# Turning z by VectorE blocks and strided reads in a two-layer FNet/GEGLU kernel

## The chip, the cores and the metric

The kernel runs on one core of a Trainium2 chip. The metric is the device time of one execution, in microseconds (us); the median of three runs is given, and the profile is one execution on its own. Below, TensorE (PE) multiplies matrices, VectorE (DVE) and ScalarE (ACT) work on elements, GpSimd (POOL) does small work and issues stores, and SyncE (SP) issues loads.

## The reference

The input x is 2048 rows (tokens) of 512 values, float32. Four residual sublayers follow each other: mix, GEGLU, mix, GEGLU, with the same matrices in both rounds.

```
def A(x):      # mix: real part of a two-dimensional DFT, as matrix products
    a = x @ dft_hid_re.T ;  b = x @ dft_hid_im.T
    return dft_seq_re @ a - dft_seq_im @ b
def B(x):      # GEGLU, 512 -> 1792 -> 512
    return (gelu(x @ w_gate) * (x @ w_up)) @ w_down
x = x + A(layernorm(x));  x = x + B(layernorm(x))      # twice
```

## The kernel before

**Products.** A float32 product is made of three fast ones: each operand is split into a high part (copied by ScalarE, line 110) and a rest (subtracted by VectorE, line 111), and `mm3` (lines 144 to 146) adds high x high, high x low and low x high in PSUM. The large products use one level of Strassen's scheme (in Winograd's form), so operands also come as sums and differences of quarters (S1 to S4, T1 to T4).

**Tiles.** All SBUF data lives in 102 slots of 128x512 float32 (`sb.get`, `sb.put`, first in, first out), and PSUM in 8 such slots (`ps8`). Activations lie in DRAM between layers as 16 tiles of 128 rows.

**Order.** A Tile scheduler places the instructions of each engine, starting from the order in which the program issues them; on the chip each engine then runs its list in order. Two lists in the program matter here:

- The *stream*: matrix tiles in the order of use. `take()` gives the next item, keeps items split 5 ahead (`AHEAD`) and loads issued 4 further ahead (`RAW`), all on SyncE's queue (line 210).
- The *queue*: small steps of side work. `step()` runs one after each stream item of a mix (six matmuls) or each down product of a GEGLU pass (twelve matmuls).

**Mix** (layers 0 and 2). Row blocks b of 512 rows pass through the stages A11, A12, S2, S3, A22 (`six`, six matmuls an item; S2 and S3 have 16 items each, the others 8), and the hidden DFT (`hid_groups`). In the last row block the order is S2, S3, A22 and then the hidden groups.

**GEGLU** (layers 1 and 3). Two passes w of 1024 rows each. A pass multiplies the transposed rows z^T (as blocks B11, B21, B22, T1 to T4, all split) by the gate and up weights in 14 steps, `up`. The down products of the pass's first 512 rows lag six steps behind; then come the last six of those and fourteen for its second 512 rows.

**Around the change.** `block_steps(layer, w)` makes the steps that prepare z^T for a pass: eight `norm(i)` steps (lines 368 to 384: statistics and scale on VectorE, a power on GpSimd, z on ScalarE), four `first(c)` and four `second(c)` steps that turn 128 columns of z each by TensorE (line 454: four 128x128 transposes into one PSUM slot, with an identity), copy and split the result and form differences, and ten steps that form T4 and split T1 to T4. For the first pass they enter the queue at S3 of the mix's last row block (line 606), for the second pass after the first half of the first pass's down products (line 876). A loop at the end of the pass (line 887) empties the queue, two steps per product where needed.

Of the kernel before, what the change touches and what calls it, by code (L numbers as in the profile page):

```python
# [38 lines left out]
def fnet_geglu(ctx: ExitStack, tc: tile.TileContext, x_in, ws, wh, wgu, wdn, out):  # L39
# [73 lines left out]
    def split_slot(src):  # L113
        hi, lo = sb.get(F32R), sb.get(F32R)
        split(src, hi, lo)
        return hi, lo
# [20 lines left out]
    def copied(src):  # L137
        v = sb.get()
        nc.scalar.activation(v, src, AF.Copy)  # L139
        return v  # L140
# [227 lines left out]
    def normed(layer, i):  # L368
        x = fresh.pop(i, None)
        if x is None:  # L370
            x = x_load(layer, i)
        st = spool.tile([P, 6], F32, name="st")
        nc.vector.bn_stats(st, x)  # L373
        mv = spool.tile([P, 2], F32, name="mv")
        nc.vector.bn_aggr(mv, st)
        rstd = spool.tile([P, 1], F32, name="rstd")
        nc.vector.tensor_scalar_add(rstd, mv[:, 1:2], EPS)  # L377
        nc.gpsimd.tensor_tensor(rstd, rstd, power, op=ALU.pow)  # L378
        shift = spool.tile([P, 1], F32, name="shift")
        nc.vector.scalar_tensor_tensor(shift, mv[:, 0:1], -1.0, rstd, op0=ALU.mult, op1=ALU.mult)  # L380
        z = sb.get()
        nc.scalar.activation(z, x, AF.Identity, bias=shift, scale=rstd)  # L382
        sb.put(x)
        return z
# [55 lines left out]

    def block_steps(layer, w):

        z, t = {}, {}

        def norm(i):
            def run():
                z[i] = normed(layer, w * 2 * NT + i)
            return run

        def turned(c, part):  # L450

            ps = ps8.get()
            for i in range(NT):
                nc.tensor.transpose(ps[:, i * P:(i + 1) * P], z[part * NT + i][:, c * P:(c + 1) * P], ident)  # L454
            if c == ND - 1:
                sb.put(*(z.pop(part * NT + i) for i in range(NT)))
            return ps

        def difference(a, b):
            v = sb.get()  # L460
            minus(v, a, b)
            return v

        def first(c):
            def run():
                ps = turned(c, 0)
                t[f"B{1 + c // 2}1", c % 2] = copied(ps)
                blocks[f"B{1 + c // 2}1", c % 2] = split_slot(ps)
                ps8.put(ps)
            return run  # L470

        def second(c):
            def run():
                ps = turned(c, 1)
                if c < 2:
                    t["B12", c] = copied(ps)
                    t["T1", c] = difference(ps, t["B11", c])
                    sb.put(t.pop(("B11", c)))
                else:
                    c0 = c - 2  # L480
                    t["T2", c0] = difference(ps, t["T1", c0])
                    t["T3", c0] = difference(ps, t["B12", c0])
                    sb.put(t.pop(("B12", c0)))
                    blocks["B22", c0] = split_slot(ps)
                ps8.put(ps)
            return run

        def fourth(c):
            def run():
                t["T4", c] = difference(t["B21", c], t["T2", c])  # L490
                sb.put(t.pop(("B21", c)))
            return run

        def divide(name, c):
            def run():
                blocks[name, c] = split_slot(t[name, c])
                sb.put(t.pop((name, c)))
            return run

        one = [norm(i) for i in range(NT)] + [first(c) for c in range(ND)]  # L500
        two = [norm(i) for i in range(NT, 2 * NT)] + [second(c) for c in range(ND)]
        two += [fourth(c) for c in range(2)]
        two += [divide(name, c) for name in ("T2", "T3", "T1", "T4") for c in range(2)]
        return one + two


    def mix(layer):
# [70 lines left out]
                    cs[0, c] = v  # L578
            ps8.put(*side)

        chains, sides, us, ws4 = {}, {}, {}, {}

        def s2(b):
            last, fore = b == NB - 1, b < FORE[layer]
            if fore:
                chains[b] = [ps8.get() for _ in range(2)]
                if b:
                    sums[b] = [fetched((layer, b, c)) for c in range(2)]
                    cs.update({(0, c): fetched((layer, b, c, "sum")) for c in range(2)})
            chain, side = chains[b], [ps8.get() for _ in range(2)]  # L590
            sides[b] = side
            if last and layer == 0:
                queue.extend(weight_steps(0))
            for second, k in skewed():
                if second:
                    six(side, "T1", k, k == 0, k == NK - 1, "T12" if last else None)
                else:
                    six(chain, "T2", k, fore and k == 0, k == NK - 1)
            us[b] = [based(b, c, p) for c, p in enumerate(chain)]
            ws4[b] = [based(b, c, p) for c, p in enumerate(side)]  # L600

        def s3(b):
            last = b == NB - 1
            chain, side, u, w4 = chains[b], sides.pop(b), us.pop(b), ws4.pop(b)
            if last:
                queue.extend(block_steps(layer + 1, 0))
                if layer == 0:
                    queue.extend(weight_steps(1))
            for second, k in skewed():
                if second:  # L610
                    six(side, "B22", k, False, k == NK - 1, "2" if last else None)
                else:
                    six(chain, "T3", k, False, k == NK - 1)
                if not second and k == NK - 1:
                    for c in range(2):
                        plus(w4[c], w4[c], chain[c])
                        cs[1, 2 + c] = w4[c]
            for c in range(2):
                plus(u[c], u[c], side[c])
                cs[0, 2 + c] = u[c]  # L620
            ps8.put(*side)
# [32 lines left out]
    def weight_steps(n):  # L654

        src, v = [], {}

        def load():
            src.extend(sb.get() for _ in range(4))
            for i, names in enumerate((*pieces[:3], ("S4", "A21"))):  # L660
                for name, h in zip(names, half):
                    v[name] = src[i][:, h]
            with tc.issue_after(stream["last"].ins):
                nc.sync.dma_start(src[0], wgu[n, :, :512])
                nc.sync.dma_start(v["A22"], wgu[n, :, 512:768])
                nc.sync.dma_start(v["A21"], wgu[n, :, 768:])

        def sums():
            plus(v["S1"], v["A21"], v["A22"])
            minus(v["S2"], v["S1"], v["A11"])  # L670
            minus(v["S3"], v["A11"], v["A21"])
            minus(v["S4"], v["A12"], v["S2"])

        def divide(i):
            def run():
                to = wblocks[n][:, i * 1024:min((i + 1) * 1024, 7 * 512)]
                p = wparts.setdefault(n, {"tiles": []})
                if i < 3:
                    t = split_slot(src[i])
                    kept(to, t)  # L680
                    for name, h in zip(pieces[i], half):
                        p[name] = (t[0][:, h], t[1][:, h])
                else:
                    t = (split_side(v["S4"]),)
                    nc.gpsimd.dma_start(to, f32(t[0]))
                    p["S4"] = (t[0][:, half[0]], t[0][:, half[1]])
                p["tiles"] += t
                sb.put(src[i])
            return run

        return [load, sums] + [divide(i) for i in range(len(pieces))]
# [36 lines left out]
    def geglu(w, layer):  # L728
# [46 lines left out]
        def first(n):  # L775
            if n < NF:
                chain[n] = ps8.get()
                product(n, chain[n], "A11", "B11", True, True)
                c11[n] = copied(chain[n])
# [85 lines left out]
        for bc in list(blocks):  # L865
            sb.put(*blocks.pop(bc))
        load_rows(0)
        if before_mix:
            queue.extend((lambda k=k: first_rows(layer + 1, k)) for k in range(NK))
        for f in range(NF - LAG, NF):  # L870
            down(f, 0)
# [1 line left out]
        if w == 0:  # L873
            weight_load(0)
            weight_load(1)
            queue.extend(block_steps(layer, 1))
        elif before_mix:
            for k in range(NT):
                queue.append(lambda k=k: second_rows(layer + 1, k))
                queue.append(lambda k=k: combine(k))  # L880
            queue.extend((lambda k=k: combine_late(k)) for k in range(NT))
# [102 lines left out]
```

## Time and profile before

| | |
|---|---|
| median of three runs | 1668.8 us (1666.82 to 1669.08) |
| the profiled execution | 1666.76 us |
| its span, first to last instruction | 1664.9 us |
| granted TensorE clock | 0.998 |
| DMA, mean | 233 GB/s |

The profile is of one execution. A row of the groups reads: line, engine, operation, output <- inputs, shape, count | busy us, mean ns of one | idle time of the engine before them and what ended it. In a timeline, the brackets give the idle time ahead of the instruction. In the table of stages, each engine's busy time is followed by its number of instructions; then come the granted clock, the mean busy share of the 16 DMA engines and GB/s. SPq is SyncE's queue of DMA issues.

### The profile page before, as it was taken

What the parts mean: (1) busy time and instruction counts of PE and PEld (TensorE: products, weight loads), DVE (VectorE), ACT (ScalarE), POOL (GpSimd) and SP (SyncE); (2) the same over time, 40 slices, a digit from 0 to 9 for tenths busy, and PEclk for the clock granted to TensorE, in tenths of its full rate; (3) what the DMA queues carried; (4) which work ended last, traced back from release to release, by engine and by line L of the source; (5) the groups of instructions that cost most, each with busy time, mean ns of one, the idle gap of its engine ahead of it and who ended that gap; (6) DMA issues with size and microseconds to landing.
All of it is one profiled execution on the core that took longest, in us unless ns stands there. A gap on an engine that the chain in (4) does not pass through costs nothing.

```text
span 1664.9 us, 22527 instructions
## 1 busy us (share of the span) xinstructions
PE 1650.4 (99%) x7296; PEld 1359.2 (82%) x7296; DVE 1190.7 (72%) x2132; ACT 776.2 (47%) x1352; POOL 169.3 (10%) x288
## 2 busy tenths in 40 slices
PE   9999999999999999999999999999999999999999
PEld 6877788888788888888888888888888888888887
DVE  8997978687887765655898785857946556656561
ACT  7744434255565543534663333444635443444440
POOL 3212100021422110000210000000100000100000
PEclk9999999999999999999999999999999999999999
DMA  9788886778766876555665766565695559755551
GB/s 361 247 279 329 306 317 227 253 252 291 273 229 215 292 269 233 172 189 198 216 227 182 240 228 228 168 227 188 225 386 184 171 177 321 259 178 175 186 183 51
DMA packets 200726, 388.46 MB, mean 233 GB/s; under 512 B 23840, under 2 KB 27424, under 8 KB 200608
## 3 DMA queue, kind: packets, MB, share of 16 engines
q1 hardware_dynamic: 183168, 329.86, 59.1%
q0 software_dynamic: 17440, 57.16, 9.1%
q8 instruction: 58, 0.95, 0.2%
q14 instruction: 60, 0.49, 0.1%
HBM read 328.73 MB, written 58.20 MB: 232 GB/s over the span
## 4 chain that ended last, share of the span: by engine, by line
PE 93%; DVE 3%; DMA 2%; issue 1%; ACT 1%; SPq 0%; DVEq 0%; ACTq 0%
PE p L144 31%; PE p L145 30%; PE p L146 30%; DMA s<-wgu 2%; DVE s L111 1%; PE p L551 1%; PE p L454 1%; DVE s L135 1%; DMA s<-ws 1%; DVE s L132 1%; DMA s<-x 0%; DVE s L725 0%; DVE s L739 0%; DVE s L723 0%; ACT s L110 0%
## 5 line engine op out<-in xcount | busy, mean ns | idle before, releaser
L145 PE MATMUL p<-s,s 128*128 128x512 f32 x2368 | 921.7, 390 | 1.9 <-DVE s L111 1.9
L146 PE MATMUL p<-s,s 128*128 128x512 f32 x2368 | 908.6, 390 | 0.0
L144 PE MATMUL p<-s,s 128*128 128x512 f32 x2368 | 901.2, 391 | 7.0 <-DVE s L135 3.9
L110 ACT ACTIVATE s<-s 128x512 fp32r<-128x512 f32 (+1 forms) x758 | 438.0, 617 | 467.6 <-DVE s L132 98.6
L111 DVE TENSOR_TENSOR s<-s,s 128x512 fp32r<-128x512 f32 (+1 forms) x758 | 490.2, 679 | 87.1 <-ACT s L110 64.3
L144 PEld LDWEIGHTS p<-s,s 128*128 128x128 f32 x2368 | 445.0, 188 | 102.9 <-DVE s L135 5.0
L145 PEld LDWEIGHTS p<-s,s 128*128 128x128 f32 x2368 | 445.4, 188 | 95.0 <-DVE s L111 3.1
L146 PEld LDWEIGHTS p<-s,s 128*128 128x128 f32 x2368 | 445.2, 188 | 93.7 <-DVE s L111 0.7
L135 DVE TENSOR_TENSOR s<-s,p 128x512 f32<-128x512 f32 x316 | 213.0, 685 | 188.9 <-PE p L146 140.6
L139 ACT ACTIVATE s<-p 128x512 f32<-128x512 f32 x248 | 145.2, 593 | 187.4 <-PE p L146 171.4
L132 DVE TENSOR_TENSOR s<-s,s 128x512 f32<-128x512 f32 (+1 forms) x290 | 172.4, 608 | 23.4 <-DMA s<-ws 15.4
L722 ACT ACTIVATE s<-s 128x512 f32<-128x512 f32 x112 | 70.4, 630 | 91.7 <-DVE s L135 90.9
L725 DVE SCALAR_TENSOR_TENSOR s<-s,s 128x512 f32<-128x512 f32 x112 | 76.8, 690 | 38.2 <-ACT s L724 37.6
L378 POOL TENSOR_TENSOR rstd<-rstd,power 128x1 f32<-128x1 f32 x64 | 50.8, 803 | 506.7 <-DVE rstd L377 500.8
L723 DVE SCALAR_TENSOR_TENSOR s<-s,s 128x512 f32<-128x512 f32 x112 | 77.0, 690 | 33.5 <-ACT s L722 31.3
L724 ACT ACTIVATE s<-s 128x512 f32<-128x512 f32 x112 | 69.5, 627 | 25.0 <-DVE s L723 24.4
L135 DVE TENSOR_TENSOR s<-s,s 128x512 f32<-128x512 f32 (+1 forms) x78 | 50.1, 645 | 38.5 <-DMA s<-ws 22.1
L169 POOL DMA_DIRECT2D x<-s x48 | 26.1, 543 | 443.8 <-DVE s L135 440.8
L382 ACT ACTIVATE s<-s,shift,rstd 128x512 f32<-128x512 f32 x64 | 50.4, 811 | 36.5 <-DVE shift L380 32.1
L739 DVE SCALAR_TENSOR_TENSOR s<-s,s 128x512 f32<-128x512 f32 x84 | 58.0, 690 | 1.6
L197 POOL DMA_DIRECT2D wb<-s x84 | 45.2, 540 | 121.6 <-ACT s L110 85.1
L373 DVE BATCH_NORM_STATS2 st<-s 128x6 f32<-128x512 f32 x64 | 42.7, 689 | 19.8 <-DMA s<-x 19.8
(32 smaller groups left out, 254.6 us busy)
## 6 DMA issues: line engine op xcount, KB each, us to landing
s<-ws SPq DMA_DIRECT2D x432, 256.0 KB, 4.0
s<-wb SPq DMA_DIRECT2D x294, 256.0 KB, 4.1
s<-wd SPq DMA_DIRECT2D x224, 256.0 KB, 4.3
s<-x SPq DMA_DIRECT2D x126, 256.0 KB, 4.1
s<-wh SPq DMA_DIRECT2D x120, 256.0 KB, 4.8
wb<-s POOLq DMA_DIRECT2D x98, 256.0 KB, 3.5
x<-s POOLq DMA_DIRECT2D x48, 256.0 KB, 4.1
wd<-s POOLq DMA_DIRECT2D x28, 256.0 KB, 4.9
```

What stands on the lines that cost most here:

```text
L110: nc.scalar.activation(hi, src, AF.Copy)
L111: nc.vector.tensor_tensor(lo, src, f32(hi), op=ALU.subtract)
L132: nc.vector.tensor_tensor(out, a, b, op=ALU.subtract)
L135: nc.vector.tensor_tensor(out, a, b, op=ALU.add)
L139: nc.scalar.activation(v, src, AF.Copy)
L144: nc.tensor.matmul(ps, ah, bh, start=start, stop=False, skip_group_check=True)
L145: nc.tensor.matmul(ps, ah, bl, start=False, stop=False, skip_group_check=True)
L146: nc.tensor.matmul(ps, al, bh, start=False, stop=stop, skip_group_check=True)
L722: nc.scalar.activation(t, g, AF.Square)
L723: nc.vector.scalar_tensor_tensor(t, t, 1.0 / GELU_C, g, op0=ALU.add, op1=ALU.mult)
L724: nc.scalar.activation(t, t, AF.Tanh, scale=GELU_A * GELU_C)
L725: nc.vector.scalar_tensor_tensor(t, t, 1.0, g, op0=ALU.add, op1=ALU.mult)
```

## The change

z is no longer turned by TensorE. Each norm step also turns its 128x512 tile in 32x32 blocks on VectorE (`nc.vector.transpose`), which leaves every block where it was, and GpSimd's queue stores the tile in a DRAM tile `turned[part]`, 512x512. New steps `fetch(c)` read 128 columns back for both halves: per half four reads on SyncE's queue, each of 32 columns, in which 16 blocks are put side by side into 32 partitions. A read thus takes 512 pieces of 32 float32. `first` and `second` then work on the SBUF tile that was read; their copies of PSUM go away.

The steps also enter the queue in other places. For a first pass the eight norms enter at S2 of the mix's last row block, and the reads and all else at S3, behind which layer 0's weight steps stand. For a second pass everything enters ahead of the last six down products of the first half (30 steps instead of 26).

```diff
         def norm(i):
+
             def run():
-                z[i] = normed(layer, w * 2 * NT + i)
+                z, v = normed(layer, w * 2 * NT + i), sb.get()
+                nc.vector.transpose(v, z)
+                part, n = divmod(i, NT)
+                nc.gpsimd.dma_start(turned[part][n * P:(n + 1) * P], v)
+                sb.put(z, v)
             return run
-        def turned(c, part):
-
-            ps = ps8.get()
-            for i in range(NT):
-                nc.tensor.transpose(ps[:, i * P:(i + 1) * P], z[part * NT + i][:, c * P:(c + 1) * P], ident)
...
+        def fetch(c):
+
+            def run():
+                for part in range(2):
+                    v = zt[c, part] = sb.get()
+                    for i in range(P // 32):
+                        cols = turned[part][:, c * P + i * 32:c * P + (i + 1) * 32]
+                        to = v[i * 32:(i + 1) * 32]
+                        nc.sync.dma_start(
+                            to.rearrange("p (j t) -> p j t", t=32), cols.rearrange("(j p) t -> p j t", p=32)
+                        )
+            return run
...
         def first(c):
             def run():
-                ps = turned(c, 0)
-                t[f"B{1 + c // 2}1", c % 2] = copied(ps)
-                blocks[f"B{1 + c // 2}1", c % 2] = split_slot(ps)
-                ps8.put(ps)
+                v = t[f"B{1 + c // 2}1", c % 2] = zt.pop((c, 0))
+                blocks[f"B{1 + c // 2}1", c % 2] = split_slot(v)
             return run
...
-        one = [norm(i) for i in range(NT)] + [first(c) for c in range(ND)]
-        two = [norm(i) for i in range(NT, 2 * NT)] + [second(c) for c in range(ND)]
+        one = [norm(i) for i in range(2 * NT)]
+        two = [fetch(c) for c in range(ND)] + [first(c) for c in range(ND)] + [second(c) for c in range(ND)]
...
-        return one + two
+        return one, two
...
         def s2(b):
...
-            if last and layer == 0:
-                queue.extend(weight_steps(0))
+            if last:
+                rows = block_steps(layer + 1, 0)
+                queue.extend(rows[0])
+                rest.extend(rows[1])
+                if layer == 0:
+                    queue.extend(weight_steps(0))
...
         def s3(b):
...
             if last:
-                queue.extend(block_steps(layer + 1, 0))
+                queue.extend(rest)
...
         load_rows(0)
-        if before_mix:
+        if w == 0:
+            queue.extend(run for part in block_steps(layer, 1) for run in part)
+        elif before_mix:
...
         if w == 0:
             weight_load(0)
             weight_load(1)
-            queue.extend(block_steps(layer, 1))
```

More of the change, by code (lines that the diff above doesn't have):

```diff
@@ L441, in block_steps @@
     def block_steps(layer, w):
-        z, t = {}, {}
+        zt, t = {}, {}
+        turned = [dram.tile([TB, D], F32, name=f"t{layer}_{w}_{part}") for part in range(2)]
         def norm(i):
             def run():
-                z[i] = normed(layer, w * 2 * NT + i)
-            return run
-        def turned(c, part):
-            ps = ps8.get()
-            for i in range(NT):
[L454 to L457, printed above, removed]
+                z, v = normed(layer, w * 2 * NT + i), sb.get()
[3 more added lines that the diff above has]
+                sb.put(z, v)
+            return run
+        def fetch(c):
[9 more added lines that the diff above has]
+            return run
         def difference(a, b):
@@ L473, in run @@
             def run():
-                ps = turned(c, 1)
+                v = zt.pop((c, 1))
                 if c < 2:
-                    t["B12", c] = copied(ps)
-                    t["T1", c] = difference(ps, t["B11", c])
+                    t["B12", c] = v
+                    t["T1", c] = difference(v, t["B11", c])
                     sb.put(t.pop(("B11", c)))
@@ L480, in run @@
                     c0 = c - 2
-                    t["T2", c0] = difference(ps, t["T1", c0])
-                    t["T3", c0] = difference(ps, t["B12", c0])
+                    t["T2", c0] = difference(v, t["T1", c0])
+                    t["T3", c0] = difference(v, t["B12", c0])
                     sb.put(t.pop(("B12", c0)))
-                    blocks["B22", c0] = split_slot(ps)
-                ps8.put(ps)
+                    blocks["B22", c0] = split_slot(v)
+                    sb.put(v)
             return run
@@ L579, in a12 @@
             ps8.put(*side)
-        chains, sides, us, ws4 = {}, {}, {}, {}
+        chains, sides, us, ws4, rest = {}, {}, {}, {}, []
         def s2(b):
```

## The prediction

> **What bounds the kernel now.** I began with the head of the page and the chain that ended last.
>
> ```profile
> span 1664.9 us, 22527 instructions
> ...
> PE 1650.4 (99%) x7296; PEld 1359.2 (82%) x7296; DVE 1190.7 (72%) x2132; ACT 776.2 (47%) x1352; POOL 169.3 (10%) x288
> ...
> PE 93%; DVE 3%; DMA 2%; issue 1%; ACT 1%; SPq 0%; DVEq 0%; ACTq 0%
> ```
>
> TensorE is busy for 99% of the span and is 93% of the chain. Whatever leaves its queue shortens the run, and whatever makes it wait lengthens it; work elsewhere counts only where it makes TensorE wait. So the second view is the timeline of TensorE, read for the idle time in brackets. Such marks are few, and the one at 552 us is the last.
>
> ```profile
> 356.62 0.50 PE L144 MATMUL p<-s,s 128*128 128x512 f32 x1 [1.02 <-DVE s L135]
> ...
> 444.55 0.50 PE L144 MATMUL p<-s,s 128*128 128x512 f32 x1 [1.85 <-ACT s L139]
> ...
> 552.40 0.50 PE L144 MATMUL p<-s,s 128*128 128x512 f32 x1 [0.18 <-ACT s L139]
> ```
>
> The first lies at the end of S2 of the last row block of layer 0, where matmuls waited for VectorE to empty an accumulator. Third comes the busy time by stage, for the stages that the change touches. Counting matmuls, I place S2 and S3 of the last row block at about 334 to 356 and 356 to 379 us in layer 0 and at 1157 to 1179 and 1179 to 1200 in layer 2, and the second half of layer 1's first GEGLU pass at 595 to 633.
>
> ```profile
> core 0: us, PE busy (x) PEld busy (x) DVE busy (x) ACT busy (x) POOL busy (x), PEclk, DMA share, GB/s
> 334.00:356.00 22.00, 21.59 (x96) 17.54 (x94) 20.95 (x37) 12.76 (x23) 5.91 (x11) 1.00 0.84 290
> 356.00:379.00 23.00, 22.38 (x107) 18.68 (x108) 19.57 (x49) 12.49 (x23) 2.98 (x5) 1.00 0.67 226
> 1157.00:1179.00 22.00, 22.00 (x99) 18.22 (x98) 22.00 (x38) 11.63 (x21) 0.00 (x0) 1.00 0.45 143
> 1179.00:1200.00 21.00, 21.00 (x102) 17.62 (x102) 18.10 (x51) 14.81 (x28) 6.16 (x8) 1.00 0.68 227
> 595.00:633.00 38.00, 38.00 (x186) 31.81 (x185) 22.87 (x51) 16.76 (x29) 3.88 (x8) 1.00 0.71 239
> 440.00:450.00 10.00, 7.12 (x23) 4.87 (x22) 10.00 (x21) 6.35 (x12) 3.76 (x7) 0.83 0.65 236
> ```
>
> In S2 VectorE is full (20.95 and 22.00 of 22 us) while TensorE hardly waits; in S3 it has some 3 us free. The last row shows what a wait costs besides itself: over these 10 us the granted clock was 0.83, so 1.7 us were lost on top of 2.88 us of idling. From 99 matmuls in 22.00 us comes the pitch of one, 0.22 us.
>
> **Removed: the transposes.** There are 128. Their own duration is no price, since matmuls overlap; the price is the pitch.
>
> ```profile
> 371.30 0.39 PE L145 MATMUL p<-s,s 128*128 128x512 f32 x1
> 371.52 0.39 PE L146 MATMUL p<-s,s 128*128 128x512 f32 x1
> 371.76 1.47 PE L454 MATMUL p<-ident,s 128*128 128x128 f32 x12
> 372.98 0.48 PE L144 MATMUL p<-s,s 128*128 128x512 f32 x1
> 373.30 0.60 PE L454 MATMUL p<-ident,s 128*128 128x128 f32 x4
> ...
> L454 PE MATMUL p<-ident,s 128*128 128x128 f32 x128 | 17.0, 272 | 0.0
> ```
>
> Twelve take 372.98 - 371.76 = 1.22 us, 102 ns each, and the matmul behind the group hands over after 0.32 us instead of 0.22, so 0.10 more. 128 x 0.102 = 13.1 us, and with some 14 such groups 1.4 us more: **14.5 us** leave the queue that bounds the kernel, a quarter of it in each of four places (A and B: before the first and the second GEGLU pass of layer 1; C and D: the same of layer 3). [...]
>
> Six PSUM copies per block also leave ScalarE, and the PSUM slots of the transposes come free. ScalarE is busy for 47%, so I book nothing for it. The splits and differences that remain read SBUF instead of PSUM: nothing.
>
> **Added on VectorE: 64 transposes; and norms move.** The trace has no such VectorE instruction. The nearest are 128x512 operations on the same engine:
>
> ```profile
> L373 DVE BATCH_NORM_STATS2 st<-s 128x6 f32<-128x512 f32 x64 | 42.7, 689 | 19.8 <-DMA s<-x 19.8
> ...
> L375 DVE BATCH_NORM_AGGREGATE mv<-st 128x2 f32<-128x6 f32 x64 | 10.3, 176 | 0.1
> L380 DVE SCALAR_TENSOR_TENSOR shift<-mv,rstd 128x1 f32<-128x1 f32 x64 | 9.9, 158 | 11.6 <-POOL rstd L378 11.1
> ...
> 1168.98 3.11 DVE L111 TENSOR_TENSOR s<-s,s 128x512 fp32r<-128x512 f32 x5
> ```
>
> Five splits back to back take 3.11 us, a pitch of (3.11 - 0.69) / 4 = 0.60 us. I take 0.60 for a transpose (bounds: 0.16, what a one-column operation takes, and 1.2, two passes over the data): 4.8 us per block. In A and C the norms move from S3 into S2 too, eight at 0.69 + 0.18 + 0.16 = 1.03 us, 8.2 us. So S2 gets up to 13.0 us more of VectorE in 22 us that are full. The cover is that splits are made five stream items ahead, 5 x 6 matmuls x 0.22 = 6.6 us. That leaves 20.95 + 13.0 - 22 - 6.6 = 5.4 us in A and 6.4 in C as the upper bound. The lower bound is nothing, since the order of instructions is made by a scheduler that may let norms fall behind the splits; a gain is excluded, because TensorE waits for VectorE there for only 1.02 us. I take half: **3 us each**. In B and D VectorE has 15 of 38 us free: nothing.
>
> **Added on GpSimd's queue: eight 256 KB writes per block.** Each waits for its transpose. Behind it stand the next norm's power and, in layer 0, the stores of split weights; TensorE needs none of these soon.
>
> **Added on SyncE's queue: 32 reads per block.** Each moves 64 KB as 512 runs of 128 bytes, where a load today moves 128 rows of 2 KB.
>
> ```profile
> q1 hardware_dynamic: 183168, 329.86, 59.1%
> ...
> x<-s POOLq DMA_DIRECT2D x48, 256.0 KB, 4.1
> ...
> s<-wgu SPq DMA_DIRECT2D x14, 256.0 KB, 4.7
> s<-wgu SPq DMA_DIRECT2D x28, 128.0 KB, 3.4
> ...
> 612.11 0.32 SPq L712 DMA_DIRECT2D s<-wb  x1
> ```
>
> Issue: 32 x 0.32 = 10 us of SyncE per block if the number of runs doesn't matter, four times that, 41 us, if it does. Ten fit into S3, and I take them.
>
> Transfer: a packet costs 0.591 x 16 x 1664.9 / 183168 = 0.086 us. A run of 128 bytes costs between a sixteenth of that, 5.4 ns (by bytes), and 86 ns (by count). Loads whose rows are half as long land in 3.4 instead of 4.7 us, so 2.1 us of 4.7, 45%, don't shrink with the row; put on a packet that makes 38 + 3 = 41 ns, though a part of it is latency that overlaps. I take 20 ns, between the first value and the last: 16,384 runs over 16 engines are **20 us per block** on all of them (ends 5.5 and 42, at worst 88). [...]
>
> The first read waits for the writes, 4.1 us from issue to landing. Behind it on SyncE stand the loads of the stream, which the splits on ScalarE and VectorE need, and so TensorE. In A and C S3's own transfers are 0.67 x 22 = 15 us; with 20 that is 35 against 22 and a lead of nine items (12 us): 1 us late, and with the wait for the writes **2 us each**. In B and D the reads stand in the queue of steps behind three to five products of the second half (12 matmuls, 2.7 us each), so they start about 603 us. Of the 30 us that remain, they need 20 and the stream 0.71 x 30 = 21, so the last end about 630, ten later than today's last transposes:
>
> ```profile
> 619.18 1.03 PE L454 MATMUL p<-ident,s 128*128 128x128 f32 x8
> ...
> 626.42 1.89 DVE L111 TENSOR_TENSOR s<-s,s 128x512 fp32r<-128x512 f32 x3
> ```
>
> Today the last split of B ends at 628.3, nine behind these. Nine behind 630 is 639; the next pass starts at 633 and reaches T2 and T1 after 12 matmuls (2.6 us): 3 us late, and up to 6 where stream loads go first. I take **5 us each**. C has more room, since VectorE then idles for long:
>
> ```profile
> 1236.77 2.73 DVE L135 TENSOR_TENSOR s<-s,p 128x512 f32<-128x512 f32 x4 [15.63 <-PE p L146]
> ```
>
> **The sum.** A and C 3 + 2 each, B and D 5 each: 20 us of new waits, two of them long enough to lower the clock, 2 x 1.7 = 3.4. Less 14.5: +8.9 us. The profiled execution took 1666.76 us (span 1664.9 and 1.9 around it), so 1675.7; the median of the runs shown is 2.0 above it: **1678 us**.
>
> **Rivals.** *Everything is covered* (faster). A run costs 5 to 10 ns, the reads take 6 to 10 us per block and fit into the free 0.3 of the DMA engines; the lead of 6.6 us and norms that fall behind hide the load of S2. 14.5 less some 2 us of waits: 1656. For it: no wait of TensorE after 552 us, and the 15.63 us of C. Against it: VectorE at 22.00 of 22. [...]
>
> *The short runs choke the queue* (far slower). At 41 ns, or with issues of 1.3 us, A and C lose 42 + 15 - 34 = 23 us each, B and D 5 + 22 = 27 each: 100 - 14.5, 1754. It decides from about 25 ns on. For it: the half rows above. Against it: their 45% hold latency. [...]
>
> *They cancel*: 11 to 18 us of waits, within 0.2% (3.3 us, about what a measurement of this kernel can tell from no change).
>
> That transposes stay on TensorE is excluded: the only line that issued them goes.
>
> **How the numbers follow.** My forecast, with its own range of 1672 to 1706: 0.42. Covered 0.36, cancelled 0.08, choked 0.14. The likeliest gives 1678. From 1655 (nearly all of the 14.5 kept) to 1708, little more than the choked case is left out. Faster 0.36, same 0.08, slower 0.42 + 0.14 = 0.56.
>
> **What would show it.** No L454 on TensorE, and its idle marks back: ended by VectorE or ScalarE, at the ends of S2 in layers 0 and 2 and at the starts of the second GEGLU passes. Packets under 512 bytes up by 65,536, and the share of q1 up by 4 x 20 us, 4.8% of the span, besides what the stream has; 1.3% would be the price by bytes, 10% the choke. VectorE up by 38 us. If no idle mark stands after 552 us, I have put the covers too low, and the first rival holds.

## The result and the profile after

The changed kernel takes 1694.72 us (median of five runs, 1692.39 to 1697.53), against 1668.8 us before (1665.17 to 1669.48 on the same chip): 1.016 of the time before, 95% interval 1.0145 to 1.0175. It is slower by 26 us, where +9 was forecast. The profiled execution took 1694.84 us, its span 1693.1.

The head of the page of the changed kernel, as shown for the kernel before:

```profile
span 1693.1 us, 22583 instructions
...
PE 1651.6 (98%) x7168; PEld 1351.2 (80%) x7168; DVE 1207.8 (71%) x2164; ACT 767.7 (45%) x1328; POOL 188.5 (11%) x320
...
PE 67%; issue 18%; DVE 6%; DMA 6%; POOL 1%; ACT 1%; SPq 1%; DVEq 0%; POOLq 0%; ACTq 0%
```

Two subtractions tell where the 28.2 us of span come from. Span less busy TensorE is 1693.1 - 1651.6 = 41.5 us and was 1664.9 - 1650.4 = 14.5: 27.0 us of new waits. And TensorE has 128 instructions less, worth the 14.5 us of the prediction, but is busy for 1.2 us more: the 7,168 that remain took 15.7 us longer. The clock says the same: 0.989 of 1693.1 is a loss of 18.6 us, 0.998 of 1664.9 one of 3.3, so 15.3 more. 27.0 + 15.3 - 14.5 = 27.8, against 28.2 measured. So the gain came, and the waits, with a lower clock beside them, took it three times over.

Where the waits are is seen in TensorE's timeline of the changed kernel (in brackets the idle time ahead):

```profile
350.49 2.08 PE L144 MATMUL p<-s,s 128*128 128x512 f32 x4 [5.30 <-ACT s L110]
355.88 0.80 PE L145 MATMUL p<-s,s 128*128 128x512 f32 x1 [3.31 <-DVE s L111]
...
394.01 2.05 PE L144 MATMUL p<-s,s 128*128 128x512 f32 x4 [4.92 <-DMA s<-wh]
...
1199.95 0.79 PE L145 MATMUL p<-s,s 128*128 128x512 f32 x1 [3.69 <-DVE rstd L377]
...
1232.98 0.50 PE L144 MATMUL p<-s,s 128*128 128x512 f32 x1 [2.62 <-ACT s L110]
...
1499.63 0.50 PE L144 MATMUL p<-s,s 128*128 128x512 f32 x1 [1.60 <-DMA s<-wb]
```

All but the last belong to A and C, the places before the first GEGLU passes. The table of stages, with A in the first two rows, C in the third, then B and D (columns as in the prediction):

```profile
345.00:380.00 35.00, 22.17 (x76) 16.14 (x76) 33.00 (x68) 21.04 (x37) 9.93 (x18) 0.80 0.82 245
380.00:400.00 20.00, 15.08 (x57) 11.96 (x56) 13.60 (x22) 6.41 (x12) 0.54 (x1) 0.83 0.91 260
1180.00:1217.00 37.00, 27.42 (x88) 18.70 (x87) 31.91 (x71) 20.95 (x35) 12.27 (x16) 0.82 0.70 184
...
610.00:680.00 70.00, 70.00 (x310) 57.91 (x309) 45.44 (x85) 30.30 (x51) 8.62 (x16) 1.00 0.92 290
1450.00:1520.00 70.00, 68.40 (x302) 56.30 (x302) 45.41 (x74) 32.53 (x55) 5.39 (x10) 1.00 0.83 251
```

In A TensorE idles for 12.8 + 4.9 = 17.7 us at a clock of 0.80 to 0.83; in C for 9.6 us, and 2.6 more at 1232.98. In B it never waits, and in D for 1.6 us. The same comes out when the n-th matmul of lines 144 to 146 is set beside the n-th of the kernel before: across A the changed kernel falls back by 20.6 us, across C by 16.7; across B it gains 3.6 and across D 3.7, a quarter of the 14.5 each, of which D gives 1.9 back at the wait of 1499.63.

Why TensorE waits in A is read from three engines. First VectorE of the changed kernel, at the first of the new norms:

```profile
327.76 0.69 DVE L111 TENSOR_TENSOR s<-s,s 128x512 fp32r<-128x512 f32 x1
330.26 0.70 DVE L373 BATCH_NORM_STATS2 st<-s 128x6 f32<-128x512 f32 x1 [1.81 <-DMA s<-x]
...
332.11 0.16 DVE L380 SCALAR_TENSOR_TENSOR shift<-mv,rstd 128x1 f32<-128x1 f32 x1 [0.75 <-POOL rstd L378]
333.15 0.71 DVE L450 STREAM_TRANSPOSE s<-s 128x512 f32<-128x512 f32 x1 [0.88 <-ACT s L382]
333.79 0.65 DVE L111 TENSOR_TENSOR s<-s,s 128x512 fp32r<-128x512 f32 x1
```

The split (L111) behind the norm shows no wait of its own; it stands behind what the norm waited for: its load of x (1.81 us), GpSimd's power (0.75) and ScalarE's z (0.88). From one split to the next 6.0 us pass, 3.4 of them idle, at the head of a stage in which VectorE had been busy for 20.95 of 22 us. ScalarE of the changed kernel has the same, some 10 us later:

```profile
339.56 0.64 ACT L110 ACTIVATE s<-s 128x512 fp32r<-128x512 f32 x1 [0.33 <-PE p L145]
343.77 0.82 ACT L382 ACTIVATE s<-s,shift,rstd 128x512 f32<-128x512 f32 x1 [3.58 <-DVE shift L380]
...
349.31 2.17 ACT L110 ACTIVATE s<-s 128x512 fp32r<-128x512 f32 x4
```

ScalarE stands for 3.58 us in front of a norm's scale, and the copies (L110) for which TensorE stands until 350.49 come four in a row from 349.31 on. By the profile's releasers, though, what held the first of these copies to the end was VectorE, whose sum of line 132 was done at 349.17. It follows a sum of line 135 that began when a load of the stream landed:

```profile
346.90 0.69 DVE L135 TENSOR_TENSOR s<-s,s 128x512 f32<-128x512 f32 x1 [0.23 <-DMA s<-ws]
...
348.48 0.69 DVE L132 TENSOR_TENSOR s<-s,s 128x512 f32<-128x512 f32 x1
```

So late loads have a share in this wait. Third, SyncE's queue, of the kernel before and then of the changed one:

```profile
329.06 16.01 SPq L210 DMA_DIRECT2D s<-ws  x8
347.00 0.33 SPq L162 DMA_DIRECT2D s<-x  x1
```

```profile
328.90 7.12 SPq L162 DMA_DIRECT2D s<-x  x5
340.84 0.33 SPq L210 DMA_DIRECT2D s<-ws  x1
...
378.67 8.47 SPq L464 DMA_DIRECT2D s<-t  x16
387.24 1.38 SPq L210 DMA_DIRECT2D s<-ws  x3
388.71 4.15 SPq L210 DMA_DIRECT2D s<-wh  x8
```

Before, eight loads of the stream (ws) were issued from 329 us on and the norms' x came after. Now five loads of x stand ahead, and the next ws is issued 12 us later; 4.8 of the 12 are a wait for a store of x (x<-s), whose slot the load is given. At 378.67 sixteen of the new reads take 8.47 us of SyncE, 0.53 us each, and behind them come the loads of wh: that is the wait of 4.92 us at 394.01.

The reads themselves are not dear. The DMA lines and the group of the new VectorE transposes of the changed kernel:

```profile
DMA packets 270871, 405.24 MB, mean 239 GB/s; under 512 B 91936, under 2 KB 95520, under 8 KB 270752
...
q1 hardware_dynamic: 250752, 338.26, 62.2%
...
s<-t SPq DMA_DIRECT2D x128, 64.0 KB, 2.6
...
L450 DVE STREAM_TRANSPOSE s<-s 128x512 f32<-128x512 f32 x32 | 22.0, 699 | 2.7 <-ACT s L382 2.5
```

Packets of q1 rose by 250,752 - 183,168 = 67,584, and its time by 0.622 x 1693.1 - 0.591 x 1664.9 = 69.1 us of all 16 engines: 17 us per block, 16.4 ns per packet. That is the whole price, and only part of it lies in the runs: by the trace's own packet records the 65,536 packets of 128 bytes took 13.1 ns each on average, 53.7 us of 16 engines, and the rows of 2 KB went from 96.6 to 98.0 ns, 14.2 us more. A read of 512 runs landed in 2.6 us, the median of 128.

### The profile page after: what moved, and what is told of

Its sections match the earlier page's. It is cut to its first block, busy times and chain, and to the rows that moved or that the text cites. A ratio compares the mean times of both kernels' runs of the same rounds, so it can differ in the third digit from the quotient of the medians.

```text
span 1693.1 us, 22583 instructions
## 1 busy us (share of the span) xinstructions
PE 1651.6 (98%) x7168; PEld 1351.2 (80%) x7168; DVE 1207.8 (71%) x2164; ACT 767.7 (45%) x1328; POOL 188.5 (11%) x320
## 3 DMA queue, kind: packets, MB, share of 16 engines
q1 hardware_dynamic: 250752, 338.26, 62.2%
## 4 chain that ended last, share of the span: by engine, by line
PE 67%; issue 18%; DVE 6%; DMA 6%; POOL 1%; ACT 1%; SPq 1%; DVEq 0%; POOLq 0%; ACTq 0%
PE p L144 22%; PE p L145 22%; PE p L146 22%; DVE s L111 2%; DMA s<-ws 2%; DVE s L132 2%; DMA s<-wgu 1%; DVE s L135 1%; DMA s<-x 1%; DMA s<-wb 1%; PE p L559 1%; DVE st L373 1%; SPq L464 1%; ACT s L110 1%; DMA x<-s 0%
## 5 line engine op out<-in xcount | busy, mean ns | idle before, releaser
L110 ACT ACTIVATE s<-s 128x512 fp32r<-128x512 f32 (+1 forms) x782 | 451.1, 617 | 534.7 <-DVE s L132 116.5
L111 DVE TENSOR_TENSOR s<-s,s 128x512 fp32r<-128x512 f32 (+1 forms) x782 | 503.1, 674 | 106.2 <-ACT s L110 77.3
L135 DVE TENSOR_TENSOR s<-s,p 128x512 f32<-128x512 f32 x316 | 212.0, 682 | 165.5 <-PE p L146 119.7
L132 DVE TENSOR_TENSOR s<-s,s 128x512 f32<-128x512 f32 (+1 forms) x314 | 187.0, 609 | 37.5 <-DMA s<-ws 18.1
L139 ACT ACTIVATE s<-p 128x512 f32<-128x512 f32 x224 | 131.2, 593 | 144.2 <-PE p L146 136.9
L736 ACT ACTIVATE s<-s 128x512 f32<-128x512 f32 x112 | 69.9, 628 | 26.4 <-DVE s L735 25.6
L135 DVE TENSOR_TENSOR s<-s,s 128x512 f32<-128x512 f32 (+1 forms) x78 | 49.7, 639 | 40.9 <-DMA s<-ws 25.5
L382 ACT ACTIVATE s<-s,shift,rstd 128x512 f32<-128x512 f32 x64 | 50.0, 808 | 37.1 <-DVE shift L380 36.8
```

What stands on the lines that cost most here:

```text
L110: nc.scalar.activation(hi, src, AF.Copy)
L111: nc.vector.tensor_tensor(lo, src, f32(hi), op=ALU.subtract)
L132: nc.vector.tensor_tensor(out, a, b, op=ALU.subtract)
L135: nc.vector.tensor_tensor(out, a, b, op=ALU.add)
L736: nc.scalar.activation(t, t, AF.Tanh, scale=GELU_A * GELU_C)
```

## The experiments

My theory after the comparison: A and C lose because norms and transposes were put into S2, where VectorE is full, and because of the reads in S3; B and D cost nothing. Most kernels below change one thing of the changed kernel; e1, e5 and e11 are edits of the kernel before, and e12 joins two. "Idle" is span less busy TensorE of the profiled execution; all ratios are to the kernel before, run beside it. "A + C" and "B + D" are the us that the profiled execution loses against the kernel before in these places (-: gains), with the n-th matmul of lines 144 to 146 set beside the n-th: A from 325 to 420 us of the kernel before, C from 1150 to 1240 (from 290 and 1132 in e6, e7 and e12), B from 595 to 720, D from 1400 to 1495.

The kernels ran on several chips, and the kernel before has medians from 1664.0 to 1668.8 us on them. A difference of two ratios is therefore a comparison across chips, uncertain by some 0.2%, or 3 to 4 us.

| kernel | median us | ratio, 95% | idle us | clock | A + C | B + D |
|---|---|---|---|---|---|---|
| before | 1668.8 | 1 | 14.5 | 0.998 | 0 | 0 |
| after | 1694.72 | 1.016, 1.0145 to 1.0175 | 41.5 | 0.989 | 37.3 | -5.3 |
| e1_place | 1673.97 | 1.0045, 1.0031 to 1.0059 | 21.3 | 0.996 | 15.7 | 0.1 |
| e2_rows | 1677.95 | 1.0073, 1.0053 to 1.0093 | 32.3 | 0.993 | 26.4 | -7.2 |
| e3_noturn | 1688.98 | 1.0145, 1.0124 to 1.0166 | 36.6 | 0.990 | 27.5 | -0.8 |
| e4_s3 | 1685.49 | 1.0115, 1.0088 to 1.0143 | 34.3 | 0.989 | 24.6 | -3.9 |
| e5_second | 1663.89 | 0.9985, 0.9976 to 0.9994 | 15.5 | 1.000 | 0.2 | -4.0 |
| e6_early | 1674.37 | 1.0045, 1.0031 to 1.006 | 30.5 | 0.995 | 15.5 | -5.2 |
| e7_spread | 1677.72 | 1.0068, 1.0056 to 1.008 | 32.9 | 0.996 | 13.2 | 0.7 |
| e8_twice | 1701.88 | 1.0223, 1.021 to 1.0236 | 48.6 | 0.987 | 43.5 | -2.3 |
| e9_later | 1685.67 | 1.0131, 1.0115 to 1.0146 | 33.6 | 0.994 | 17.2 | 3.2 |
| e10_pool | 1725.99 | 1.0366, 1.0348 to 1.0384 | 62.5 | 0.983 | 54.3 | 7.3 |
| e11_second_pool | 1678.66 | 1.0084, 1.007 to 1.0098 | 26.9 | 0.995 | -0.4 | 12.3 |
| e12_both | 1678.37 | 1.0085, 1.0069 to 1.01 | 33.5 | 0.996 | 13.7 | 2.0 |

**e1_place: the new place alone.** TensorE turns z as before, but the norms of a first pass enter at S2 and the steps of a second pass ahead of the last six down products, as in the changed kernel.

```diff
+        one = [norm(i) for i in range(2 * NT)]
+        two = [first(c) for c in range(ND)] + [second(c) for c in range(ND)]
...
+                rows = block_steps(layer + 1, 0)      # in s2, last row block
+                queue.extend(rows[0])
+                rest.extend(rows[1])
```

> TensorE still turns z; only the places change: eight norms enter the queue at S2 of the mix's last row block (A, C) and everything of a second pass ahead of the last six down products (B, D). If the loss of A and C (24 and 20 us of waits) comes from the norms' VectorE work in a stage where VectorE is full, about half of it shows here: 1680 to 1688 us, with TensorE waiting at the end of S2. If it comes from the reads or from buffers held by stores, nothing shows: 1666 to 1672 us.

Measured: 1.0045, some 7.5 us, between the two expectations. With no DMA added and no VectorE transpose, the early norms alone make TensorE wait, behind ScalarE's scale of a norm (L382). Its timeline:

```profile
355.83 1.12 PE L454 MATMUL p<-ident,s 128*128 128x128 f32 x4 [2.90 <-ACT s L382]
...
1184.33 0.98 PE L454 MATMUL p<-ident,s 128*128 128x128 f32 x4 [2.09 <-ACT s L382]
```

In B and D the new place costs nothing (0.1 us by matmuls); in A and C it costs 15.7 in this profiled execution, which was the slowest of ten. Both marks stand ahead of L454, though, TensorE's own turning, which the changed kernel no longer has: 5.0 of the 9.3 us of waits in A and C. So the early place is shown to cost something with TensorE's turning; how much of that the changed kernel pays, this run can't say.

**e2_rows: the same bytes in long rows.** Eight reads of whole 256 KB tiles per block in place of 32; the blocks are then not put into their places.

```diff
-                    for i in range(P // 32):
...
+                    nc.sync.dma_start(v, turned[part][c * P:(c + 1) * P])
```

> Each block's 32 reads of 512 runs are replaced by eight reads of a whole stored tile (128 rows of 2 KB, the same bytes), so the blocks are not put in their places and the result isn't z^T; all else stays. If the reads (issues on SyncE's queue and time of 128-byte runs, 17 us of all DMA engines per block) cause the loss, it goes: 1655 to 1668 us. If VectorE's load causes it, only the late part of A and C goes: 1682 to 1692 us.

Measured: 1.0073, so 0.87%, 14.5 us, less than the changed kernel and between the two expectations. By matmuls A and C lose 26.4 us instead of 37.3: the short runs and their 32 issues are some three tenths of that loss. The rest stays: the idle time is still 32.3 us, with the largest wait of A now behind a split.

```profile
373.76 0.80 PE L145 MATMUL p<-s,s 128*128 128x512 f32 x1 [4.62 <-DVE s L111]
```

**e3_noturn: no VectorE transpose.** z itself is stored and read; the norm takes one slot fewer. z^T is then not formed.

```diff
-                z, v = normed(layer, w * 2 * NT + i), sb.get()
-                nc.vector.transpose(v, z)
+                v = normed(layer, w * 2 * NT + i)
...
-                sb.put(z, v)
+                sb.put(v)
```

> The 32 VectorE transposes are left out (z is stored as it is, so what is read back is not z^T) and with them one slot per norm. If VectorE's load in S2 causes the loss, 5 us of it go in A and in C each: 1683 to 1688 us. If the reads cause it, nothing changes: 1692 to 1697 us. If slots that wait for stores cause it, a part goes too, and no engine should then wait for a store's landing less than now.

**e8_twice: every VectorE transpose done twice.**

```diff
                 nc.vector.transpose(v, z)
+                nc.vector.transpose(v, z)
```

> The change with every VectorE transpose done twice into the same tile: 5 us more of VectorE per block, no other buffer, load or read. If VectorE's load in S2 causes the loss of A and C, TensorE's waits grow by 4 to 8 us in each and B and D stay: 1703 to 1712 us. If the loss comes from loads that wait for slots or from the reads, it grows by less than 2 us in each: 1693 to 1698 us.

Measured: without them 1.0145, at most some 2.5 us less than the changed kernel, with intervals that overlap; with them twice 1.0223, 0.63% or 10.5 us more, with intervals far apart; the two medians differ by 7.2. Thirty-two transposes at 0.60 are 19 us of VectorE, of which half lies in A and C, 9.6. By matmuls A and C lose 6.2 us more with them twice (3.9 and 2.3), and 9.8 less without them (7.1 and 2.7). So most of what is added to VectorE there reaches the end, as the theory of a full VectorE asks, though C grows by less than the 4 to 8 us expected. That e3 gains little in all comes from B and D, which gain 0.8 us instead of 5.3, with waits for wb and for ScalarE's copies. As e3 also holds one slot fewer per norm, its 9.8 need not be VectorE's alone. The wait that grew most is the first one of A, from 5.30 to 8.96 us; of this kernel:

```profile
355.83 2.08 PE L144 MATMUL p<-s,s 128*128 128x512 f32 x4 [8.96 <-ACT s L110]
```

**e4_s3: norms back at S3**, with all else of the change.

```diff
-                queue.extend(rows[0])
-                rest.extend(rows[1])
+                rest.extend(rows[0] + rows[1])
```

> The change, but the norms of A and C enter the queue at S3 again, ahead of the reads. If the norms' place in S2 causes the loss, A and C get 8 to 10 us each back: 1674 to 1680 us. If the reads cause it, they now come 11 us later and closer to their use: 1695 to 1708 us.

Measured: 1.0115, some 7.5 us less than the changed kernel, outside both expectations: by matmuls A loses 10.1 us instead of 20.6, C 14.5 instead of 16.7. In A the waits of S2 shrink to one of 1.18 us, but now the reads come too late for the first items of the GEGLU pass, and the loss moves behind S3. Its timeline in C:

```profile
1231.47 1.65 PE L144 MATMUL p<-s,s 128*128 128x512 f32 x3 [6.51 <-ACT s L110]
```

So neither place does. My reading, which no run isolates, is that the chain of norm, transpose, store and read is longer than the turning by TensorE was, and either its head collides with S2 or its end is late.

**e5_second: B and D alone.** The first passes as before, the second as in the changed kernel.

```diff
+    def turned_steps(layer, w):        # block_steps of the changed kernel
...
-                queue.extend(rest)
+                queue.extend(block_steps(layer + 1, 0))      # that of before, at S3
...
-            queue.extend(run for part in block_steps(layer, 1) for run in part)
+            queue.extend(run for part in turned_steps(layer, 1) for run in part)
```

> Only the second passes (B, D) go by VectorE, store and reads; the first passes (A, C) keep TensorE's transposes and their old places. If the loss is that of A and C alone, B and D keep their half of the transposes' 14.5 us, less some 2 us of waits: 1660 to 1664 us, faster than both kernels. If the reads disturb what runs beside them wherever they are, it is 1668 or above.

Measured: 0.9985, interval 0.9976 to 0.9994, faster than both kernels: 2.5 us less than before, under the 0.2% that I had called distinguishable, but the interval leaves out 1. Aligned by matmuls, B and D gain 3.6 us each, and 1.8 and 1.4 are given back at the start of the next pass, where a load of wb is late. In B its SyncE queue, the last subtraction of the splits of z^T, and TensorE's first wait; then its line of q1:

```profile
605.07 21.18 SPq L530 DMA_DIRECT2D s<-t  x32
```

```profile
637.67 0.70 DVE L111 TENSOR_TENSOR s<-s,s 128x512 fp32r<-128x512 f32 x1
```

```profile
648.34 0.50 PE L144 MATMUL p<-s,s 128*128 128x512 f32 x1 [1.47 <-DMA s<-wb]
```

```profile
q1 hardware_dynamic: 216960, 334.06, 61.4%
```

Thirty-two reads hold SyncE for 21.18 us, 0.66 each, and the last split ends at 638.4, nearly where I had put it (639). Even so TensorE doesn't wait for it. The splits are made in the order T2, T3, T1, T4, as the reads land, and the pass uses T2, T1, B11, T3, B22, B21, T4: what is split last is used last. q1 gained 0.614 x 1658.3 - 984.0 = 34.2 us, 17.1 per block, the same as in the changed kernel.

**e6_early and e7_spread: more time for A and C.** In the first, norms, transposes and stores enter at A22 of the row block before the last, with the reads at S3; in the second, the reads are also spread out, four at every second step from the middle of S2.

```diff
         def a22(b):
             chain = chains.pop(b)
+            if b == NB - 2:
+                rows = block_steps(layer + 1, 0)
+                queue.extend(rows[0])
+                rest.extend(rows[1])
```

```diff
+        two = [s for c in range(ND) for part in range(2) for s in (fetch(c, part), None)] + ...
...
+                queue.extend(head + [None] * (8 - len(head)))      # in s2, last row block
+                queue.extend(rest[:16])
```

> The change, but the norms, turns and stores of A and C are done some 35 us earlier, at A22 and the hidden groups of the row block before the last, where VectorE has time; the reads stay at S3. If the norms' work in S2 is what costs, TensorE's waits in S2 and the half clock behind them go (13 us in A, 4 to 15 in C): 1665 to 1676 us. If the reads cost most, 1682 us or more.

> As the run with early norms, and the reads are spread: four of them every second step, from the middle of S2 to the middle of S3, where 32 stood in four steps. If what is left is the pile of reads in front of the stream's loads, it goes: 1655 to 1662 us. If it is the time of the short runs themselves, it stays: within 3 us of the run with early norms.

Measured: 1.0045 and 1.0068. The earlier place takes 19 us off. By matmuls (from 290 us on in A, from 1132 in C, since the work begins earlier) C now loses 4.3 and 1.8 us, where the changed kernel loses 16.7, but A still 11.3 and 11.4, of 20.6. Spreading the reads didn't help. In A the DMA engines are nearly full in e6; its stage of A and TensorE's timeline:

```profile
334.00:357.00 23.00, 17.19 (x60) 12.57 (x59) 21.87 (x40) 11.19 (x20) 7.02 (x13) 0.78 0.97 330
```

```profile
349.10 0.80 PE L145 MATMUL p<-s,s 128*128 128x512 f32 x1 [3.87 <-DVE s L111]
```

0.97 of the DMA engines against 0.84 in the kernel before, where layer 0's weight steps store and load as well. In layer 2, without these, the same edit takes most of the loss away.

**e9_later: slots.** x, z and the transposed tile hold three SBUF slots per norm until the store has read its one. The pool is first in, first out, so a load that is given such a slot waits for the norm or for the store. Here the three are given back three norms later.

```diff
-                sb.put(z, v)
+                later.extend((z, v))      # x is put there too
+                if i >= 3:
+                    sb.put(*(later.pop(0) for _ in range(3)))
```

> The change, but the three slots of a norm are given back three norms later in the program, so that the stream's loads are not put into slots that the norm's scale or the store still reads. If SyncE's waits for these (L382 and the stores' landing) are what starves VectorE and TensorE, A gets 5 us or more back and C some: 1682 to 1690 us. If they only come last by chance, the time stays within 3 us, or grows as fewer slots are free: 1692 to 1700 us.

Measured: 1.0131, 0.29% or 5 us less than the changed kernel, with intervals that all but touch; the medians differ by 9.0, and 1685.67 us is what was expected if slots starve the stream. The total hides more than it shows. By matmuls A and C lose 17.2 us instead of 37.3 (10.6 and 6.6), while B and D, which had gained 5.3, now lose 3.2, with waits of 3.11 and 2.88 us for wb at the starts of the second passes. The profiled execution was the fastest of four, 3 us under their median, which does not account for 20 us. In C the mechanism is seen too: on SyncE's queue loads of x (L162) waited for stores of turned tiles, whose slots they take over. From 1130 to 1250 us, first the changed kernel, then e9_later:

```profile
SPq L162 <- DMA t<-s: 9.8, 2, 6.5
```

```profile
SPq L162 <- DMA t<-s: 2.9, 1, 2.9
```

In A it isn't: SyncE waited 7.5 us behind lines 377 and 382 in the changed kernel and 10.1 behind line 382 and the stores here (300 to 400 us), so why A gains 10 us stays open. The scheduler also places the instructions anew after each edit, and no run separates that from the slots. Giving slots back later before the first passes alone was not run.

**e12_both: e6 and e9 together**, to tell slots from full DMA engines in what is left of A.

> The norms, turns and stores of A and C a row block earlier (as in the kernel with early norms, which took 1.0045 of before) and a norm's three slots given back three norms later (which took 5 us off the changed kernel). If what is left of A there is that loads of the stream wait for slots that the chain of norm, turn and store still holds, the two together give 1663 to 1670 us, a ratio of 0.998 to 1.002. If it is that the DMA engines are full at that place (busy share 0.97), giving the slots back later frees no transfer: 1671 to 1677 us, a ratio of 1.003 to 1.006, with the share still above 0.95.

Measured: 1.0085, slower than e6 alone and above what either gave. A loses 11.3 us by matmuls, as in e6 and e7, though the DMA share in its stage is 0.90 instead of 0.97; what came on top are waits for wb at the starts of the second passes. The stage of A in this kernel, and the waits of SyncE's queue in 300 to 380 us:

```profile
334.00:357.00 23.00, 15.70 (x56) 11.94 (x55) 21.02 (x38) 9.42 (x17) 6.93 (x13) 0.78 0.90 332
```

```profile
SPq L210 <- DMA t<-s: 9.3, 4, 3.7
```

Loads of the stream (L210) stand 9.3 us behind stores of transposed tiles, whose slots they take over: giving slots back later in the program's order moved that wait and didn't end it. C loses 2.4 us, against 4.3 in e6. So what is left of A isn't settled; neither theory gave the number.

**e10_pool and e11_second_pool: reads on GpSimd's queue**, to free SyncE: in the changed kernel, and in e5.

```diff
-                        nc.sync.dma_start(
+                        nc.gpsimd.dma_start(
```

> The change, but the reads are issued from GpSimd's queue instead of SyncE's. If what the reads cost (16.8 us by the run with whole-tile reads) is SyncE's order, the stream's loads standing behind reads that wait, most of it comes back: 1678 to 1685 us. If it is the time of the 128-byte runs on the DMA engines, or if GpSimd takes long to make 512 runs, nothing comes back: 1692 us or more.

> Only the second passes by VectorE, as before, with the reads issued from GpSimd's queue. Waits for a weight load (1.5 and 1.1 us, with the half clock behind them) follow the reads of B and D. If the loads stand behind the reads on SyncE, these waits go: 1660 to 1662 us. If the DMA engines are what is full, they stay: 1663 to 1665 us.

Measured: 1.0366 and 1.0084, both far slower than with SyncE (1.016 and 0.9985), and e11 above both of its expectations. The reads of e10_pool, the waits ahead of them, and its queue:

```profile
L464 POOL DMA_DIRECT2D s<-t x128: 648/648/684, 355.7 to 1516.5; - x128
...
  DMA s<-t: 18.8, 29
```

```profile
q0 software_dynamic: 24096, 73.95, 12.5%
...
s<-t POOLq DMA_DIRECT2D x128, 64.0 KB, 6.6
```

An issue took 0.648 us there, not more than SyncE's 0.66 in e5, but a read landed in 6.6 us instead of 2.6, and 29 of the 128 first waited for an earlier one. Here the queue was worse for latency, not for issue time. The norms' powers and the stores stand in the same list as these 128 issues (83 us of GpSimd); how much of the loss is theirs wasn't separated.

## Why the prediction was wrong in size and right in sign

The step that failed is the cover of A and C. Their waits were booked at 10 us and came to 29.9, and the clock that follows them at 3.4 and came to 15.3; B and D, booked at 10, took 1.6.

**The gain** held. B and D return 3.6 us each, a quarter of 14.5.

**VectorE in S2** was under-costed: 3 us each was booked, half of an upper bound of 5.4 and 6.4. The bound itself failed. It counted only busy time against a cover of 6.6 us, as if the new work came without waits. The norms' own waits (x, GpSimd, ScalarE) counted too, 3.44 us at the first norm alone, and ScalarE, which I had put at nothing, stood 3.58 us in front of L382 with splits behind it. The price of a norm also left out line 377, some 0.15 us each. The step on SyncE's queue was left out as well: of a norm that is moved, its loads of x move with it, ahead of the stream. e1 gives 7.5 us for the place, over half of its waits ahead of TensorE's turning; in e6, with the norms out of S2, A and C lose 21.8 us less; and e8 shows that VectorE time added there costs 6.2 us of 9.6 in A and C. The text also counted 64 VectorE transposes and +38 us; there are eight per block, 32 in all, and VectorE rose by 17.1 us. The price of one, 0.60 us of pitch, and the 4.8 us per block were right.

**Slots** were not in the sum at all: x, z and the turned tile of a norm hold three until the store has read its one, and later loads take these over. With them given back later, in e9, A and C lose 20 us less.

**The reads in A and C** were booked at 2 us each. e2 takes 14.5 us off by making them long, 10.9 of it in A and C. The packet was priced high enough (20 ns taken, 16.4 measured with all that it slows), so the transfers weren't what was mis-sized; the issue was: 0.53 us each in A instead of 0.32, 17 us of SyncE instead of 10, with the loads of wh behind it. e2 makes the runs long and the issues few at once, so that it is the issue is argued from SyncE's rows, not isolated.

**B and D** were booked at 5 us each and cost 0 and 1.6. The last split comes as late as I had worked out, but I set it against the need of T2, the first of the blocks that are used, and it is T4 that is split last and used six products later. The rival in which everything is covered was right for this half, and e5 gives its gain alone.

**The clock** was booked at 3.4 us and took 15.3. By its factor this is the term most mis-sized. I counted two places of one wait each; there are seventeen in A and C, sixteen of them in stretches of 20 to 37 us at a clock of 0.80 to 0.83.

The sum of waits, 27.0 against 20, was thus near by errors that cancel: B and D too dear by 8, A and C too cheap by 20 (17.7 and 12.2 against 5 each), and some 4.6 us of waits gone in other places, 2.9 of them around 444 us. The *choked* rival falls: it needed 25 ns a run or issues of 1.3 us, and in the trace a run took 13.1 ns and an issue 0.487 us in the median. The rival in which everything is covered had 5 to 10 ns a run; 5.4, by bytes, was worked out from the trace, and no run shows the 10. The 86 ns was itself a mean over all packets of q1, among them 20,352 of 4 bytes; a row of 2 KB alone took 96.6 ns.

**Shown and not shown.** Shown: the norms' place costs (e6), the short reads with their issues cost (e2), VectorE time in S2 costs (e8), B and D are covered (e5). Shown in its size, and only in C in its way: when a norm's slots come free (e9). Only argued: how the 37.3 us of A and C divide among VectorE's and ScalarE's order, SyncE's and the slots. The edits don't add up: by matmuls e2, e3, e6 and e9 each take 10 to 22 us off A and C, 63 us together, so each wait removed lets another come last. Open: what holds A in e6, e7 and e12, and why A gains in e9.

## What to carry to other kernels

Work taken off the bounding engine paid here only where the replacement's whole chain, with its own loads, stores and waits, started late enough not to disturb and ended early enough to be ready; that held before the second passes (gains of 3.6 and 3.7 us) and not before the first (losses of 20.6 and 16.7), and doing only the half that fits came out 0.15% ahead of the kernel before. When a step is moved into a full stage, price its waits on every engine that it visits, not only its busy time. Price the clock by how long a stretch of waits lasts, not by the number of waits: here it was 0.80 to 0.83 over stretches of 20 to 37 us. And read an experiment place by place: e9's total looked like 5 us, and was 20 us gained in two places and 8.5 lost in two others.

## What the runs showed of the hardware

- A read of 512 runs of 128 bytes on SyncE's queue took 0.303 us to issue at best, 0.53 to 0.66 in a row, and 13.1 ns of one DMA engine per run, 16.4 with what it added to other packets. The time of a packet wasn't the same in every run, though: in e10_pool q1 carried the same 183,168 packets as before and took 0.593 x 1726.3 = 1023.7 us of the engines instead of 984.0.
- On GpSimd's queue the same 128 reads were counted as 24,096 - 20,000 = 4,096 packets, by the trace's records 2,048 of 4 KB and 2,048 of 4 bytes, and landed in 6.6 us instead of 2.6.
- Short waits were followed by a lower clock of TensorE. In the kernel before three idle marks of 0.47, 1.85 and 0.56 us within 5 us are followed by matmuls at a pitch of 0.43 us, where it was 0.22 to 0.23 ahead of them; the granted clock of 440 to 450 us was 0.83. Not every wait had this behind it: in e5_second TensorE waited 2.3 us for VectorE (L135), 1.5 for a load of wb and 1.4 for ScalarE (L139), each the longest of its kind, and the granted clock of the whole profiled execution was 1.000. The kernel before:

```profile
445.61 0.79 PE L144 MATMUL p<-s,s 128*128 128x512 f32 x1 [0.56 <-DVE s L135]
...
447.06 0.63 PE L144 MATMUL p<-s,s 128*128 128x512 f32 x1
447.48 0.63 PE L145 MATMUL p<-s,s 128*128 128x512 f32 x1
```
